# Gate, up and convolution matmuls as ordered 64-row pairs on TensorE, with norm statistics split between VectorE and GpSimd

## The chip, the cores and the metric

The kernel runs on one core of a Trainium2 chip. A core has TensorE (PE, matmuls; its weight loads are listed apart as PEld), VectorE (DVE), ScalarE (ACT), GpSimd (POOL), and SyncE (SP), from whose queue nearly all transfers are issued. The metric is the device time of one execution in microseconds (us), lower is better.

## The reference

For 2048 rows of 576 numbers in bfloat16, the reference computes an adaptive-norm block with a long convolution, and then a gated feed-forward part:

```python
mod = (silu(c) @ w_mod).reshape(1, 6, 1, -1)        # sa, ca, ga, sb, cb, gb
h = layernorm(q) * (1 + ca) + sa
kv = shift(k, shift_k) * v                          # four taps per channel
y = irfft(rfft(kv, 4096) * rfft(ssm_k, 4096))[:2048] + kv * ssm_D
x = q + ga * (h * y)
h = layernorm(x) * (1 + cb) + sb
x = x + gb * ((silu(h @ w1) * (h @ w3)) @ w2)       # w1, w3: 576 x 4608, w2: 4608 x 576
```

The Fourier transforms are the reference's way to a causal convolution over the 2048 positions, one filter per channel. The norms have no weights of their own, and divide by sqrt(variance + 1e-5).

## The kernel before

**Tiling.** The rows are cut into eight blocks of 256 for the convolution (`s` = 0 to 7) and four blocks of 512 for the feed-forward part (`r` = 0 to 3; block r holds convolution blocks 2r and 2r+1). The convolution is done by blocks: short Fourier transforms of each block of kv (`X`) and of the filter (`V`, from spectra `W`) as matmuls with a cosine and sine basis, products and sums of spectra on VectorE (`pair`, L403), and an inverse transform by matmuls (`inverse`, L533). Spectra that are needed again later are written to DRAM by `keep_x` and `keep_v` (L418, L422) and read back by `get` (L433); all of these are issued from SP.

**Feed-forward.** The 4608 hidden columns are 36 tiles of 128, taken in nine chunks of four (`fc`). The contraction over 576 channels is four tiles of 128 rows and one of 64 rows. An item is one hidden tile over 512 rows (or two hidden tiles over 256 rows): gate and up products go into the two banks of one PSUM tile, ScalarE takes silu of the first (L939) and copies the second (L941, tile `u`), and VectorE multiplies them into `h` (L942, all three in `hide`). The PSUM pool has four such tiles in rotation, and the convolution takes its own PSUM tiles from the same pool (`ps`, L70). The remaining 64 rows of w1 and w3 lie in one weight tile, w1's in partitions 0 to 63 and w3's in 64 to 127[...].

**`stream`** (L885) runs the gate and up products for r = 0, 1 and 2, in pairs of items: the 16 matmuls of 128 rows of the early item (`full`), its two 64-row matmuls (`rest`), the two 64-row matmuls of the late item, and the 16 of 128 rows of the late item. After each item `advance` (L874) lets the convolution of the next row block come in, piece by piece. It is a chain of generators, each piece yielding what it is supposed to cost; a budget grows with every item by a rate derived from `CONV_US` (72, 97 and 108 us for r = 0, 1, 2). A negative yield is a distance that other pieces are to fill (`mix`, L721). Before r = 0's stream stands the first block, written out in order (`first_block`, L632); then `stream` runs 24 hidden tiles on the first 256 rows with block 1's convolution beside it (`conv_second`, L781), then the rest of r = 0.

**`stream_halves`** (L975) runs r = 3, which has no convolution beside it. Every matmul has 64 rows. A pair is one matmul on rows 0 to 63 into one bank and one on rows 64 to 127 into the other; after five pairs the banks are swapped, and four pairs follow. Both halves of the rows thus accumulate in each bank, one after the other. The swapped part of an item runs after the first part of the next item, and its order behind the first part is kept by a memset on GpSimd that waits for the first part and is waited for by the second:

```python
nc.gpsimd.memset(self.tok[:], 0.0)          # L993
marks[f] = newest()
self.wait_for(marks[f], first)
```

**`down`** (L1014) multiplies h by w2 for each row block and adds into the output rows.

**Weights.** `load_w13` (L865) loads one chunk of w1 and w3: two transfers of 512 KB and two of 64 KB. Two buffers alternate, and a load waits until the chunk before last has been used.

**Norm statistics.** ScalarE makes the sums and the sums of squares (`ln_sums`, L441); `ln_scales` (L455) turns them into a scale and a shift for each row in five small operations, all on GpSimd. `gate_stats` (L488) does this for the first norm, `ln_stats` (L447) for the second. `normed_act` (L566) then writes the normed rows, `turn` (L573) transposes them on TensorE, and `turned` (L597) brings them to the feed-forward's input. `k_rows` (L359) transposes the filter rows in the same way.

**Order.** The instructions stand on each engine in the order in which the program issues them, except where `behind` (L483) or `issue_after` places one behind another. Waits between engines are by semaphore.

## Time and profile before

The three runs took 521.01, 521.48 and 522.43 us.

| | us |
|---|---|
| median of three runs | 521.48 |
| profiled execution, whole | 520.93 |
| profiled execution, span | 518.7 |
| TensorE busy | 498.0 |
| TensorE weight loads busy | 295.0 |
| VectorE busy | 339.7 |
| ScalarE busy | 294.1 |
| GpSimd busy | 72.0 |
| gate and up, 128-row matmuls (L920), 1056 | 200.7 |
| gate and up, 64-row matmuls beside them (L931), 264 | 33.1 |
| gate and up of r = 3, 64-row matmuls (L987), 648 | 70.3 |
| down matmuls (L1032), 1152 | 146.7 |

The granted TensorE clock was 0.996 on the mean. The span is from the first to the last recorded instruction; 2.2 us of the profiled execution lie around it. Busy times of matmuls are of overlapping instructions, so that the mean of one is longer than the distance from one to the next. In the lines of the timeline and of the chain, the columns are start in us, duration in us, engine, line and operation, the output tile and its inputs, and `x16` for a run of sixteen; `[1.03 <-ACT u L941]` says that the engine stood idle for 1.03 us before, until the instruction named.

### The profile page before, as it was taken

Reading aid. Unit: us, or ns where it says so; the run is one execution under the profiler, and the core shown is the slowest. Engines: PE = TensorE matmul, PEld = TensorE weight load, DVE = VectorE, ACT = ScalarE, POOL = GpSimd, SP = SyncE. Lnnn points to the kernel's source line nnn. Section 1 sums busy time; section 2 is a strip of 40 time slices with the busy share of each in tenths; the row PEclk is TensorE's granted clock in tenths of the full one; section 3 lists DMA queues with packets and bytes.
Section 4 is the critical chain, followed back from the end, with each engine's and each line's share of the span. In section 5 each row is a group of like instructions: output and inputs, shape, how many; then the busy total and the mean of one; then the engine's idle time right before and its main releaser. Section 6 shows DMA issues by size and latency. Waiting matters only on the chain.

```text
span 518.7 us, 9266 instructions
## 1 busy us (share of the span) xinstructions
PE 498.0 (96%) x3650; PEld 295.0 (57%) x3650; DVE 339.7 (65%) x515; ACT 294.1 (57%) x581; POOL 72.0 (14%) x131
## 2 busy tenths in 40 slices
PE   6998999988899999999999999999999999999996
PEld 3666875455587544444677643434578644444775
DVE  8897899997895445798999636999761222222012
ACT  5757789665652367858643465886725355555000
POOL 3304005107012001100102000530101000000000
PEclk9999999999899999999999999999999999999999
DMA  8947869678679966467997649855555545532462
GB/s 273 321 148 207 265 226 285 198 249 255 198 233 322 299 194 224 112 233 252 368 300 243 183 124 365 309 184 141 156 138 141 157 122 161 174 115 71 117 180 69
DMA packets 102206, 107.80 MB, mean 208 GB/s; under 512 B 5075, under 2 KB 94228, under 8 KB 102164
## 3 DMA queue, kind: packets, MB, share of 16 engines
q1 hardware_dynamic: 102142, 107.21, 66.3%
q8 instruction: 28, 0.46, 0.4%
q14 instruction: 14, 0.11, 0.1%
q10 hardware_dynamic: 22, 0.01, 0.0%
HBM read 96.00 MB, written 11.21 MB: 207 GB/s over the span
## 4 chain that ended last, share of the span: by engine, by line
PE 69%; DVE 17%; DMA 5%; ACT 4%; POOL 2%; issue 1%; SPq 0%; POOLq 0%; ACTq 0%
PE ps L1032 25%; PE ps L920 20%; PE ps L987 12%; DMA wst<-in_B_w_dram 4%; PE ps L931 3%; DVE p L413 2%; DVE z L415 2%; DVE h L942 2%; PE ps L302 2%; POOL l2v L460 2%; PE ps L543 2%; DVE kv L338 1%; PE ps L316 1%; ACT junk L445 1%; DVE kvt L337 1%
## 5 line engine op out<-in xcount | busy, mean ns | idle before, releaser
L920 PE MATMUL ps<-h2T,wst 128*128 128x512 bf16 (+1 forms) x1056 | 200.7, 341 | 1.0 <-ACT W L318 0.8
L1032 PE MATMUL ps<-wst,h 128*128 128x288 bf16 x1152 | 146.7, 288 | 2.4 <-ACT u L941 1.2
L920 PEld LDWEIGHTS <-wst 128*128 128x128 bf16 x1056 | 100.2, 98 | 85.8 <-issue 14.0
L1032 PEld LDWEIGHTS <-h 128*128 128x128 bf16 x1152 | 112.9, 98 | 33.0 <-issue 3.9
L939 ACT ACTIVATE h<-ps 128x512 bf16<-128x512 f32 x108 | 64.9, 601 | 69.1 <-PE ps L931 41.9
L942 DVE TENSOR_TENSOR h<-h,u 128x512 bf16<-128x512 bf16 x108 | 45.0, 421 | 42.2 <-ACT u L941 42.2
L987 PE MATMUL ps<-h2T,wst 64*128 64x512 bf16 x648 | 70.3, 376 | 0.2 <-DMA wst<-in_B_w_dram 0.2
L941 ACT CAST u<-ps 128x512 bf16<-128x512 f32 x108 | 63.4, 587 | 0.0
L413 DVE TENSOR_TENSOR p<-X,V 128x3456 bf16<-128x3456 bf16 x28 | 54.7, 1954 | 8.9 <-DMA X<-Xd 6.4
L415 DVE TENSOR_TENSOR z<-z,p 128x3456 bf16<-128x3456 bf16 x28 | 54.7, 1954 | 0.2
L987 PEld LDWEIGHTS <-wst 64*128 64x128 bf16 x648 | 31.4, 94 | 38.9 <-DMA wst<-in_B_w_dram 0.7
L1002 DVE TENSOR_TENSOR h<-h,u 128x512 bf16<-128x512 bf16 x36 | 15.3, 425 | 55.4 <-ACT u L1001 55.4
L1049 DVE TENSOR_TENSOR og<-ps,gbrow 128x288 bf16<-128x288 f32 x32 | 13.2, 450 | 48.8 <-PE ps L1032 48.8
L999 ACT ACTIVATE h<-ps 128x512 bf16<-128x512 f32 x36 | 21.5, 598 | 36.6 <-PE ps L987 36.6
L445 ACT ACTIVATE junk<-x 128x576 bf16<-128x576 bf16 x54 | 37.1, 688 | 0.5
L460 POOL TENSOR_TENSOR l2v<-l2s 128x2 f32<-128x2 f32 x6 | 14.7, 2456 | 156.4 <-ACT junk L445 156.4
L460 POOL TENSOR_TENSOR l1v<-l1s 128x2 f32<-128x2 f32 x7 | 17.8, 2544 | 127.3 <-ACT junk L445 127.3
L931 PE MATMUL ps<-h2T,wst 64*128 64x512 bf16 (+1 forms) x264 | 33.1, 342 | 0.0
L605 ACT ACTIVATE h2T<-ps,sbcol,cbcol 128x256 bf16<-128x256 bf16 x35 | 16.8, 570 | 23.4 <-PE ps L575 23.4
L570 ACT ACTIVATE h2row<-x,l2n,l2r 128x576 bf16<-128x576 bf16 (+1 forms) x24 | 13.8, 652 | 17.1 <-POOL l2n L464 17.1
L1001 ACT CAST u<-ps 128x512 bf16<-128x512 f32 x36 | 20.9, 580 | 0.0
L931 PEld LDWEIGHTS <-wst 64*128 64x128 bf16 x264 | 8.5, 94 | 21.2 <-issue 20.8
(142 smaller groups left out, 431.0 us busy)
## 6 DMA issues: line engine op xcount, KB each, us to landing
wst<-in_B_w_dram SPq DMA_DIRECT2D x80, 512.0 KB, 5.0
wst<-in_B_w_dram SPq DMA_DIRECT2D x72, 288.0 KB, 3.6
X<-Xd SPq DMA_DIRECT2D x8, 864.0 KB
Xd<-X SPq DMA_DIRECT2D x6, 864.0 KB, 6.1
wst<-in_B_w_dram SPq DMA_DIRECT2D x80, 64.0 KB, 3.0
kh<-in_A_k_dram SPq DMA_DIRECT2D x7, 720.0 KB, 7.2
Vd<-V SPq DMA_DIRECT2D x4, 864.0 KB
V<-Vd SPq DMA_DIRECT2D x4, 864.0 KB, 8.4
```

The lines of the kernel that those rows point to most:

```text
L413: nc.vector.tensor_mul(p[:], X[:], V[:])
L415: nc.vector.tensor_add(z[:], z[:], p[:])
L445: self.nc.scalar.activation(junk[:], src[:, i, :], func, scale=scale, accum_out=out[:, col:col + 1])
L460: e.tensor_mul(var[:], ssum[:], ssum[:])
L920: nc.tensor.matmul(gus[k][:, i, a * n:(a + 1) * n], w[:, 5 * i + ct, (fi + a) * P:(fi + a + 1) * P], hT[:, ct, t0:t1], start=(first and ct ...
L931: nc.tensor.matmul(gus[k][:, i, a * n:(a + 1) * n], w[rows, 4, (fi + a) * P:(fi + a + 1) * P], hT[rows, 4, t0:t1], start=(first and a == 0 ...
L939: nc.scalar.activation(h3, gus[k][:, 0, :].rearrange("p (a t) -> p a t", a=m), ACT.Silu)
L941: nc.scalar.copy(u[:], gus[k][:, 1, :])
L942: nc.vector.tensor_mul(h3, h3, u[:].rearrange("p (a t) -> p a t", a=m))
L987: nc.tensor.matmul(gus[f][:, i, :], w[rows, 5 * i + ct if ct < 4 else 4, cols], hT[rows, ct, :], start=swap == 0 and ct == 0, stop=swap == ...
L999: nc.scalar.activation(h3, gus[f][:, 0, :], ACT.Silu)
L1032: nc.tensor.matmul(acc[t], self.h3[:, f0 + f, t * P:(t + 1) * P], w[:, f, :], start=(f0 + f == 0), stop=(f0 + f == NF - 1))
```

## The change

Gate and up products of all four row blocks now run in `stream`, as pairs of 64-row matmuls; `stream_halves` and the GpSimd memset are gone. An item is a first part of five pairs and, with the banks swapped, a second part of four (`part`). The first two pairs (`AHEAD`) of the next item are issued between them. The second part waits for the last matmul of the first by TensorE's own semaphore: `after` puts a no-operation with that dependency on TensorE and places the following matmul behind it.

While a stream runs (`halves` is true) the convolution's matmuls run as such pairs too (`two_banks`): first all terms with rows 0 to 63 into one bank and rows 64 to 127 into the other, then the same swapped, behind a wait. In between, `pause` ends the present round of `advance`, so that part of an item comes in between. `advance` is called twice an item, with half the budget each. The transposes of filter rows and of normed rows become 64 by 64 transposes, two for each of 128 rows, into two banks, and the copies out of PSUM follow that layout; the filter rows need two copies instead of one. In the first block and beside the down products the former 128-row matmuls remain.

The norm's small operations are split. `ln_var` makes the variance with two VectorE operations and leaves the power to GpSimd; `ln_shift` makes the shift with one VectorE operation, and is called later. The new calls of `gate_var` stand after the filter or kv pieces.

Left out of the diff below: the removed bodies, which are shown above, constants that are not used any more, and calls whose arguments alone change.

```diff
+AHEAD = 2
...
+    def newest(self):
+        return self.nc.cur_bb.bb.instructions[-1]
+
+    def after(self, first):
+
+        with self.behind(self.nc.tensor):
+            nop = self.nc.tensor.nop().ins
+            self.tc.add_manual_dep(
+                nop, first.name,
+                mybir.DependencyInfo(mybir.DependencyClass.Sync, mybir.DependencyReason.DATA),
+                reason="both halves of the rows write this bank, one after the other")
+        return self.tc.issue_after(nop)
+
+    def two_banks(self, outs, terms):
+
+        mm = self.nc.tensor.matmul
+        if not self.halves:
+            for n, term in enumerate(terms):
+                for i in range(2):
+                    mm(outs[i], *term(i, slice(0, P)), start=(n == 0), stop=(n == len(terms) - 1))
+            return
+        for swap in range(2):
+            with self.after(mark) if swap else nullcontext():
+                for n, term in enumerate(terms):
+                    for rows, i in ((slice(0, 64), swap), (slice(64, P), 1 - swap)):
+                        mm(outs[i], *term(i, rows), start=(swap == 0 and n == 0),
+                           stop=(swap == 1 and n == len(terms) - 1))
+            if swap == 0:
+                mark = self.newest()
+                self.pause = True
+                yield 0.0
...
+                def term(cc):
+                    return lambda h, rows: (basis[rows, cc * (e + 1), cs], rhs[rows, cc, h * H:(h + 1) * H])
                 ps = self.ps()
-                for cc in range(2):
-                    for h in range(2):
-                        nc.tensor.matmul(ps[:, h, 0:H], basis[:, cc * (e + 1), cs],
-                                         rhs[:, cc, h * H:(h + 1) * H],
-                                         start=(cc == 0), stop=(cc == 1))
+                yield from self.two_banks([ps[:, h, 0:H] for h in range(2)], [term(cc) for cc in range(2)])
...
+        if self.halves:
+            for cc in range(2):
+                for ct in range(5):
+                    for half in range(2 if ct < 4 else 1):
+                        rows, at = slice(64 * half, 64 * half + 64), 320 * cc + 64 * ct
+                        nc.tensor.transpose(pt[:, half, at:at + 64], nat[rows, ct, cc:B:2],
+                                            self.ident[rows, rows])
+            for half, n in ((0, 5), (1, 4)):
+                nc.scalar.copy(_ap(kT, 64 * half, [[D, 2], [P, n], [1, 64]]),
+                               _ap(pt, 1024 * half, [[320, 2], [64, n], [1, 64]]))
+        else:
+            for cc in range(2):
+                for ct in range(5):
+                    nc.tensor.transpose(pt[:, cc, ct * P:(ct + 1) * P], nat[:, ct, cc:B:2],
+                                        self.ident[:])
+            nc.scalar.copy(kT[:], pt[:, :, 0:D])
...
-    def ln_stats(self, src, name):
-
-        ssum = self.small.tile([P, 2], F32, name=name + "s", tag="ssum")
-        ssq = self.small.tile([P, 2], F32, name=name + "q", tag="ssq")
-        for i in range(2):
-            self.ln_sums(src, i, ssum, ssq)
-        return self.ln_scales(ssum, ssq, name)
-
-    def ln_scales(self, ssum, ssq, name):
-        small = self.small
+    def ln_var(self, ssum, ssq, name):
         n = ssum.shape[-1]
-        var, rstd, nmr = [small.tile([P, n], F32, name=name + k, tag=f"ln{k}{n}") for k in "vrn"]
-        e = self.nc.gpsimd
+        var, rstd = [self.small.tile([P, n], F32, name=name + k, tag=f"ln{k}{n}") for k in "vr"]
+        e = self.nc.vector
         e.tensor_mul(var[:], ssum[:], ssum[:])
-        e.tensor_sub(var[:], ssq[:], var[:])
-        e.tensor_single_scalar(var[:], var[:], EPS, op=ALU.add)
-        e.tensor_tensor(rstd[:], var[:], self.neghalf[:, 0:n], op=ALU.pow)
-        e.tensor_mul(nmr[:], ssum[:], rstd[:])
+        e.scalar_tensor_tensor(var[:], ssq[:], EPS, var[:], op0=ALU.add, op1=ALU.subtract)
+        self.nc.gpsimd.tensor_tensor(rstd[:], var[:], self.neghalf[:, 0:n], op=ALU.pow)
+        return ssum, rstd, name
+
+    def ln_shift(self, ssum, rstd, name):
+        n = ssum.shape[-1]
+        nmr = self.small.tile([P, n], F32, name=name + "n", tag=f"lnn{n}")
+        self.nc.vector.tensor_mul(nmr[:], ssum[:], rstd[:])
         return rstd, nmr
...
+        self.l1[s] = ssum, ssq, "l1"
+
+    def gate_var(self, s):
+        self.l1[s] = self.ln_var(*self.l1[s])
 
     def gate_rows(self, s):
 
         x1 = self.xo[s]
-        r, b = self.l1.pop(s)
+        r, b = self.ln_shift(*self.l1.pop(s))
...
+            for half in range(2):
+                rows, at = slice(64 * half, 64 * half + 64), 320 * cc + 64 * ct
+                self.nc.tensor.transpose(pt[:, half, at:at + 64], self.h2row[rows, cc, cols],
+                                         self.ident[rows, rows])
...
-                    r, b = self.ln_stats(self.xo[s], "l2")
-                yield -waits[2]
+                    for i in range(2):
+                        self.ln_sums(self.xo[s], i, *sums)
+                yield -waits[2] / 2
+                stats = self.ln_var(*sums, "l2")
+                yield -waits[2] / 2
+                r, b = self.ln_shift(*stats)
...
         yield from self.v_block(1)
+        self.gate_var(1)
         yield from self.pair(self.X[0], self.V[1], 1)
...
             yield from self.kv_rows(s0)
+            self.gate_var(s0)
...
             yield from self.pair(X0, self.V[s1], s1)
+            self.gate_var(s1)
             self.gate_rows(s0)
...
+            if self.pause:
+                self.pause = False
+                break
...
+        def part(k, swap, some=slice(None)):
             (fc, t0, t1, _, _), fi, m = items[k]
             w, n = ws[fc, t0, t1], t1 - t0
+            terms = [(ct, a) for ct in ((0, 1, 2, 3) if swap else (4, 0, 1, 2, 3)) for a in range(m)]
+            for ct, a in terms[some]:
+                cols = slice((fi + a) * P, (fi + a + 1) * P)
+                for rows, i in ((slice(0, 64), swap), (slice(64, P), 1 - swap)):
                     nc.tensor.matmul(gus[k][:, i, a * n:(a + 1) * n],
-                                     w[rows, 4, (fi + a) * P:(fi + a + 1) * P], hT[rows, 4, t0:t1],
-                                     start=(first and a == 0), stop=(not first and a == m - 1))
+                                     w[rows, 5 * i + ct if ct < 4 else 4, cols], hT[rows, ct, t0:t1],
+                                     start=swap == 0 and (ct, a) == terms[0],
+                                     stop=swap == 1 and (ct, a) == terms[-1])
+            return self.newest()
...
+            if k == len(items):
+                return
             if items[k][1] == 0:
                 load(items[k][0])
             gus[k] = self.ps()
-        for k in range(0, len(items), size):
-            early, late = range(k, k + size // 2), range(k + size // 2, k + size)
-            for m in early:
-                begin(m)
-                full(m, True)
-            for m in early:
-                rest(m, False)
-            for m in late:
-                begin(m)
-                rest(m, True)
-            for m in early:
-                hide(m)
-            if finish and late.stop == len(items):
+            part(k, 0, slice(0, AHEAD * items[k][2]))
+        self.halves = True
+        begin(0)
+        for k in range(len(items)):
+            if finish and k + 1 == len(items):
                 self.end()
-            for m in late:
-                full(m, False)
-                hide(m)
-
-    def wait_for(self, later, first):
-
-        self.tc.add_manual_dep(
-            later, first.name,
-            mybir.DependencyInfo(mybir.DependencyClass.Sync, mybir.DependencyReason.DATA),
-            reason="both halves of the rows write this bank, one after the other")
-
-    def stream_halves(self, r):
-
-        nc = self.nc
-        hT = self.h2T[r % 2]
-        newest = lambda: nc.cur_bb.bb.instructions[-1]
-        gus, ws, marks = {}, {}, {}
-
-        def part(f, swap):
-            w = ws[f // FC]
-            cols = slice(f % FC * P, (f % FC + 1) * P)
-            for ct in range(4 if swap else 5):
-                for rows, i in ((slice(0, 64), swap), (slice(64, P), 1 - swap)):
-                    nc.tensor.matmul(gus[f][:, i, :], w[rows, 5 * i + ct if ct < 4 else 4, cols], hT[rows, ct, :],
-                                     start=swap == 0 and ct == 0, stop=swap == 1 and ct == 3)
-                    if swap == 1 and ct == 0 and i == 1:
-                        self.wait_for(newest(), marks.pop(f))
-            if swap == 0:
-                first = newest()
-                nc.gpsimd.memset(self.tok[:], 0.0)
-                marks[f] = newest()
-                self.wait_for(marks[f], first)
-
-        def hide(f):
-            h3 = self.h3[:, f, :]
-            nc.scalar.activation(h3, gus[f][:, 0, :], ACT.Silu)
-            u = self.hp.tile([P, RB], BF16, name="u", tag="u")
-            nc.scalar.copy(u[:], gus.pop(f)[:, 1, :])
-            nc.vector.tensor_mul(h3, h3, u[:])
-        for f in range(NF + 1):
-            if f < NF:
-                if f % FC == 0:
-                    self.load_w13(f // FC, (r + f // FC) % 2)
-                    ws[f // FC] = self.w13.pop(f // FC)
-                gus[f] = self.ps()
-                part(f, 0)
-            if f > 0:
-                part(f - 1, 1)
-                hide(f - 1)
+            mark = part(k, 0, slice(AHEAD * items[k][2], None))
+            self.advance(rate * 2.05 * 0.5)
+            begin(k + 1)
+            with self.after(mark):
+                part(k, 1)
+            hide(k)
+            self.advance(rate * 2.05 * 0.5)
+        self.halves = False
...
-            if r == NRB - 1:
-                self.stream_halves(r)
-            else:
-                self.stream(r, jobs, rate, 2)
+            self.stream(r, jobs, rate)
```

## The prediction

> **What bounds the kernel now.** I read the page's busy shares first, then the windows by stage, the chain of waits, and the timeline around the places that change. The page:

> ```profile
> span 518.7 us, 9266 instructions
> PE 498.0 (96%) x3650; PEld 295.0 (57%) x3650; DVE 339.7 (65%) x515; ACT 294.1 (57%) x581; POOL 72.0 (14%) x131
> ```

> TensorE is busy 96% of the span, but 96% is a mean. The windows by stage (columns: stretch, its length, then PE, PEld, DVE, ACT and POOL busy, granted clock, DMA share, GB/s), for most of the r=0 stream, then all of the r=1, r=2 and r=3 streams:

> ```profile
> 65.50:127.00 61.50, 57.86 (x436) 35.57 (x436) 61.11 (x83) 45.53 (x93) 18.59 (x12) 1.00 0.76 238
> 167.00:252.00 85.00, 84.16 (x451) 37.07 (x450) 59.05 (x84) 60.18 (x121) 6.35 (x15) 1.00 0.72 233
> 291.00:372.00 81.00, 80.20 (x417) 33.74 (x416) 59.97 (x84) 55.25 (x110) 11.97 (x11) 1.00 0.65 213
> 408.60:479.00 70.40, 70.16 (x650) 31.38 (x648) 16.15 (x41) 37.06 (x70) 3.17 (x36) 1.00 0.44 134
> ```

> In r=0 it is VectorE that is full (61.11 of 61.5); TensorE has 3.6 us to spare. In r=1 and r=2 TensorE is full and VectorE has over 20 us to spare. r=3 already runs as 64-row pairs.

> The chain of waits gives the price of an item in both forms:

> ```profile
> 215.60 3.56 PE ps L920 x16
> 219.70 3.56 PE ps L920 x16
> 223.79 3.56 PE ps L920 x16
> 431.61 47.66 PE ps L987 x440
> ```

> In r=1 two items take 223.79 - 219.70 = 4.09 us, 2.05 us each. In r=3, 220 pairs take 47.66 us, 216.6 ns a pair, so an item of nine pairs takes 1.95 us. The lines of the 128-row matmuls leave 4.09 - 3.56 = 0.53 us for two pairs (0.43 us) and 0.10 us over. The start-to-start times there show the 0.10: 96 ns at each change between 128-row and 64-row work, and little else.

> [...] a two-element multiply on POOL took 8.21 us while VectorE was full:

> ```profile
> 118.66 8.21 POOL L460 TENSOR_TENSOR l2v<-l2s 128x2 f32<-128x2 f32 x1 [25.81 <-ACT junk L445]
> 127.53 0.72 POOL L463 TENSOR_TENSOR l2r<-l2v,neghalf 128x2 f32<-128x2 f32 x1
> 128.56 2.29 ACT L570 ACTIVATE h2row<-x,l2n,l2r 128x576 bf16<-128x576 bf16 x4 [6.36 <-POOL l2n L464]
> 131.85 0.75 PE L367 MATMUL ps<-ident,knat 128*128 128x128 bf16 x10 [4.29 <-ACT u L941]
> ```

> **Part 1: mode changes go.** Between 33 and 372 us I count 56 changes into 64-row work at 96 ns (5.4 us) and as many back: 10.7 us, about 3.2 in r=0, 3.5 in r=1, 3.5 in r=2. In r=0 they lie under VectorE: worth 0 (3.2 if VectorE were not full). In r=1 and r=2 they lie on the path: -7.0.

> **Part 2: the wait of TensorE on itself.** A matmul's update comes 391 ns after its start (512 columns) and a waiting weight load goes 42 ns later: 0.43 us in all. In the new order two pairs of the next item (AHEAD = 2) and any piece of convolution stand between the mark and the waiting part, 0.55 to 0.77 us of work. So it costs 0; what queues behind it is all of TensorE. Were it late by 73 ns on each of some 144 items, it would eat all 10.7 us. For the first part of a convolution pair `yield 0.0` with `pause` puts half an item in between: 0 too.

> **Part 3: PSUM tiles come back later.** This is the charge that the change does not announce. The pool has four tiles in rotation. Before, an item's tile was asked for again with over 2 us of TensorE work in between. Now the lead pairs of item k+2 are issued right after the first part of k+1, and a convolution piece is let in at every half item; where item, convolution, item, convolution alternate, the tile for the lead of k+2 is that of item k. Between the last matmul of item k and that lead stand three pairs (0.65 us) and two half pieces of convolution (0.48 us at 120 ns a 288-column pair): 1.11 to 1.13 us. What has to happen meanwhile: matmul end 0.39, ScalarE's start 0.06, silu to cast 0.49 (below), cast 0.58, release 0.04, in all 1.55 us. The wait is 0.44 us.

> ```profile
> 300.50 0.60 ACT L939 ACTIVATE h<-ps 128x512 bf16<-128x512 f32 x1 [0.94 <-PE ps L920]
> 300.99 0.58 ACT L941 CAST u<-ps 128x512 bf16<-128x512 f32 x1
> ```

> Going through the new order tile by tile: six such places in r=1 and one of 0.19, 2.8 us; in r=2 two of 0.44 and four of 0.19 to 0.32, 1.7 us; in r=0 3.1 us, hidden by VectorE. Where ScalarE also runs a statistics pass (0.69 us) in front, more: up to 2 us. I take +4.5 (bounds 3 to 8).

> **Part 4: weights are wanted sooner.** The lead of the next chunk's first item needs w1 and w3 both, before the last part of the present chunk; before, w1 alone was needed first, and w3 some 0.9 us later. The window from release to need shrinks by 1.9 us. A chunk lands 5.9 us after its release, 7.7 with a spilled V before it on SP's queue, 9.2 with an X between. In r=1 one or two chunks fall short: +1 (0 to 2). In r=2 SP's queue now stands so:

> ```profile
> 307.83 1.11 SPq L872 DMA_DIRECT2D wst<-in_B_w_dram  x2
> 308.99 0.58 SPq L438 DMA_DIRECT2D X<-Xd  x1
> 309.67 0.93 SPq L871 DMA_DIRECT2D wst<-in_B_w_dram  x2
> 310.65 0.88 SPq L438 DMA_DIRECT2D V<-Vd  x1
> ```

> In the new order two chunks have an X and a V (864 KB each) ahead of them, where now one X lies between: 3.4 us later at these rates. The path allows for part of it; +3 (0 to 8). Against it, TensorE's 1.5 us of idle time at 370 to 372 us, behind ScalarE's statistics, may shrink: -0.5.

> **Part 5: r=0.** VectorE sets the pace. The four tiles of block 1's spectrum are now spread over item halves (2.1 us in one go before, about 5.9), which puts VectorE idle by some 4 us before the X sums. GpSimd's 8.21 us at 118.66 becomes three VectorE operations of 0.15 us and one power of 0.7: up to 4.3 us gained at 131.85, the wait shown above. But VectorE waits for the power, as the next tiny multiply stands right behind (0.8 us, some five times), and once its first multiply stands about 2.5 us ahead of ScalarE's sums. I take +0.8 for the stage (-2 to +7).

> **Part 6: small things.** Half transposes, 18 or 20 of 64x64 where 10 full ones took 0.56 us: -0.3 to +0.3 a set; kT copied by two ScalarE passes in place of one of 1.13 us: +0.3 in all. First block: ScalarE's wait for GpSimd's statistics (2.2 us) goes, but TensorE holds the path there: -0.3. r=3: the GpSimd memset that ordered the halves cost nothing (it waited with 1.8 us to spare); -0.2. The down stages are untouched.

> **The sum.** -7.0 + 4.5 + 1 + 3 - 0.5 + 0.8 + 0.3 - 0.3 - 0.2 = +1.6, and +0.5 as a share of the ScalarE collisions of part 3 that I could not place: +2.1. The profiled execution took 520.93 us, of which 518.7 is the span; it lies 0.55 under the median of 521.48. 521.48 + 2.1 = 523.6; I forecast 523.5 us.

> **The rivals.**
> (a) Faster. [...] PSUM waits at their low end (3), no DMA wait, -2 in r=0: -7.0 + 3 - 0.5 - 2 - 0.2 = -6.7, about 515. It decides once weights arrive in the shorter window (parts 4 under 1 us), and r=0 keeps its POOL gain. For it: the 96 ns are real, and DMA share is 0.65 to 0.72 in r=1 and r=2. Against: the rotation of four tiles is arithmetic.
> (b) No change. VectorE and ScalarE hold r=0 and the end of r=2 (the chain of waits runs over VectorE from 341 to 366 us), so that the gain lives in r=1 alone and the PSUM waits eat it: -3.5 + 2.8 + 0.5 = about 521.3.
> (c) Much slower. A late chunk in r=2 delays items, these delay u and h, VectorE's products start late, and the end of the stream moves with them; with +8 for DMA and +5 in r=0: about 531. For it: at 332.98 the chain already holds 2.02 us of waiting for weights.
> [...]

> **How the numbers follow.** Chances: my forecast with its neighbourhood (+0.3% to +1%, 523 to 527) 0.35, (a) 0.27, (b) 0.20, (c) 0.18. About 0.3% (1.6 us) is what a measurement of this kernel can tell from no change. Slower: 0.35 + 0.18 = 0.53; same 0.20; faster 0.27. The likeliest case's own range is 522 to 527; the range over all cases is 515.5 to 530: it leaves out about one in ten below, where (a) comes with all its gains, and one in ten above.

> **What would show it.** Right: items in r=1 without a convolution beside them at 1.95 us; the 96 ns steps gone; some ten TensorE waits of 0.2 to 0.5 us released by the cast of u in r=1 and r=2; a TensorE wait on weights in r=2 near 315 to 335 us; no POOL operation of several us in the statistics. Wrong: TensorE waits in r=1 and r=2 under 2 us in all (then a), or waits of the second parts on TensorE itself, which I put at 0, or VectorE in r=0 idle by more than 5 us (then c).

## The result, and the profile after

The changed kernel takes 572.12 us (569.82 to 574.86 over four runs) where the kernel before takes 521.25 us in the same comparison: 1.098 times as long (95% interval 1.092 to 1.103). The forecast was 523.5 us in a range from 515.5 to 530; its direction was right, its size was not.

One sentence of the description above has to be corrected. On the engines the instructions do not simply stand in the order in which the program issues them: outside the first block a scheduler of the framework sorts them by its own reckoning of when each can start, and only what `behind`, `issue_after` or a data dependency ties down stays. That matters below.

The page of the changed kernel:

```profile
span 570.0 us, 11683 instructions
PE 506.5 (89%) x4891; PEld 323.4 (57%) x4892; DVE 347.7 (61%) x557; ACT 297.6 (52%) x586; POOL 21.6 (4%) x39
```

TensorE's share falls from 96% to 89%, while its matmuls at full clock take the same time (table below). GpSimd's busy time falls from 72.0 to 21.6 us, as meant. The windows of the four streams, with the columns of the table of before:

```profile
65.50:155.00 89.50, 69.43 (x932) 49.78 (x926) 72.62 (x112) 56.77 (x114) 4.65 (x5) 0.92 0.60 189
196.00:284.00 88.00, 78.51 (x733) 40.60 (x731) 56.68 (x90) 59.47 (x118) 2.06 (x3) 0.98 0.61 197
331.00:423.00 92.00, 80.83 (x733) 41.05 (x730) 62.63 (x93) 57.93 (x115) 2.06 (x3) 0.94 0.55 181
460.60:530.00 69.40, 69.40 (x644) 31.10 (x645) 15.96 (x40) 37.32 (x70) 0.00 (x0) 1.00 0.45 136
```

In r=0 VectorE is no longer full (72.6 of 89.5), in r=1 and r=2 TensorE has 9 to 11 us of gaps, and its granted clock is 0.92 to 0.98 in all three. Only r=3 is as good as before. TensorE's waits by line and releaser (us in all, times, longest), the five largest that concern the streams and the down stages:

```profile
PE ps L983 <- ACT u L995: 16.5, 16, 3.6
PE ps L983 <- DMA wst<-in_B_w_dram: 11.8, 9, 1.8
PE ps L618 <- DVE h2row L518: 6.7, 3, 5.2
PE ps L1038 <- DMA wst<-in_B_w_dram: 5.5, 3, 4.8
PE ps L97 <- ACT u L995: 4.3, 4, 1.7
```

Before, no wait of TensorE in r=1 and r=2 came to 1 us.

From the start of each matmul (a pair counted as one) to the start of the next, less the matmul's own time (the median at full clock from one such matmul to the next in these two traces: 216 ns for 512 columns, whether one 128-row matmul or a pair of 64 rows, and 122 in the one and 123 in the other for 288), the span divides as follows, to about 1 us. "Half clock" is time lost where a matmul takes twice its time (427 ns for a pair of 512 columns, 240 for 288 columns), in the stretches where the trace shows a granted clock of one half and at the very start; "waits" are gaps over 0.15 us; a change of mode is one between 128-row and 64-row matmuls.

| us | before | after | difference |
|---|---|---|---|
| matmuls at full clock, and other short gaps | 475.2 | 473.5 | -1.7 |
| waits | 17.2 | 67.6 | +50.4 |
| half clock | 4.7 | 17.9 | +13.2 |
| changes of mode (150 before, 50 after) | 14.3 | 4.6 | -9.7 |
| ahead of the first and after the last matmul | 7.3 | 6.4 | -0.9 |
| span | 518.7 | 570.0 | +51.3 |

So the change does what it says: 100 of 150 changes of mode are gone. It pays for that with 64 us of waits and half clock. By stage, each bounded by the first or last w2 matmul (r=0's stream from 33 us on), in us:

| | r=0 stream | down | r=1 stream | down | r=2 stream | down, r=3 and its down |
|---|---|---|---|---|---|---|
| before | 99.8 | 41.0 | 78.2 | 39.5 | 78.5 | 144.4 |
| after | 122.0 | 41.0 | 86.8 | 47.8 | 90.2 | 145.4 |

How a wait in r=1 comes about, on TensorE and on ScalarE of the changed kernel (timeline):

```profile
229.89 0.30 PE L97 MATMUL ps<-kv,Fb 64*128 64x288 bf16 x2
230.47 1.47 PE L983 MATMUL ps<-h2T,wst 64*128 64x512 bf16 x12 [0.27 <-ACT u L995]
232.53 0.30 PE L97 MATMUL ps<-kv,Fb 64*128 64x288 bf16 x2
235.06 2.74 PE L983 MATMUL ps<-h2T,wst 64*128 64x512 bf16 x12 [2.23 <-ACT u L995]
```

```profile
230.83 0.71 ACT L487 ACTIVATE junk<-x 128x576 bf16<-128x576 bf16 x1
...
233.27 0.68 ACT L487 ACTIVATE junk<-x 128x576 bf16<-128x576 bf16 x1
...
233.96 0.58 ACT L993 ACTIVATE h<-ps 128x512 bf16<-128x512 f32 x1
234.43 0.57 ACT L995 CAST u<-ps 128x512 bf16<-128x512 f32 x1
```

At 230.47 the lead of an item waits for the PSUM tile of the item before last; from the start of the matmul ahead (229.89) it is 0.58 us, 0.45 more than that matmul takes. At 235.06 four passes of norm statistics stood on ScalarE ahead of silu and cast, and the same wait is 2.4 us. Then the twelve matmuls take 2.74 us in place of 1.47: the granted clock is 0.50 from 234.91 to 238.32 us.

In this trace the clock is 1.00 or 0.50 wherever it is recorded, from 9.6 us on. Up to the last matmul there are ten stretches at 0.50, eight of 3.41 us and two of 6.83 us, and their starts lie whole multiples of 3.41 us apart. Cut into steps of 3.41 us from one of these starts, the two traces have 297 whole steps at full clock, the kernel before from 12.9 us on and the changed one from 9.6 us. In 11 of them, one before and ten after, TensorE was idle (no matmul in the profile) for 1.92 us or more, and each was followed by a step at half clock; in the other 286 it was idle for 1.78 us or less, and none was. The length of a single wait did not tell. A wait of 2.02 us in the kernel before, 1.17 and 0.85 us of it in two steps, was not followed by half clock (first line); one of 1.68 us in the changed kernel, in a step with 1.92 us of idle time in all, was (second line, then the windows of that step and the next):

```profile
44.51 0.77 PE L302 MATMUL ps<-kv,Fb 128*128 128x288 bf16 x5 [2.02 <-DVE kv L340]
```

```profile
130.84 0.30 PE L97 MATMUL ps<-kv,Fb 64*128 64x288 bf16 x2 [1.68 <-ACT u L995]
```

```profile
129.10:132.51 3.41, 1.49 (x22) 1.02 (x21) 3.41 (x5) 1.67 (x3) 0.00 (x0) 1.00 1.08 350
132.51:135.92 3.41, 3.41 (x24) 1.71 (x20) 3.41 (x4) 1.62 (x3) 0.00 (x0) 0.50 0.65 193
```

### The profile page after: what moved, and what is told of

Same layout as the page of the kernel before. It is cut to its first block, busy times and chain, and to the rows that moved or that the text cites. A ratio compares the mean times of both kernels' runs of the same rounds, so it can differ in the third digit from the quotient of the medians.

```text
span 570.0 us, 11683 instructions
## 1 busy us (share of the span) xinstructions
PE 506.5 (89%) x4891; PEld 323.4 (57%) x4892; DVE 347.7 (61%) x557; ACT 297.6 (52%) x586; POOL 21.6 (4%) x39
## 4 chain that ended last, share of the span: by engine, by line
PE 53%; DVE 19%; DMA 14%; ACT 10%; issue 2%; SPq 1%; POOL 0%; DVEq 0%; ACTq 0%; POOLq 0%
PE ps L983 29%; PE ps L1038 19%; DMA wst<-in_B_w_dram 9%; ACT junk L487 4%; DVE p L455 4%; DVE z L457 3%; DMA h<-in_w_mod_dram 2%; ACT u L995 2%; DVE h L996 2%; DVE kvt L368 2%; ACT h L993 2%; PE ps L91 2%; DVE kv L369 1%; DMA kh<-in_A_k_dram 1%; PE ps L284 1%
## 5 line engine op out<-in xcount | busy, mean ns | idle before, releaser
L983 PE MATMUL ps<-h2T,wst 64*128 64x512 bf16 (+1 forms) x3024 | 311.0, 357 | 32.1 <-ACT u L995 16.5
L983 PEld LDWEIGHTS <-wst 64*128 64x128 bf16 x3024 | 166.1, 97 | 158.1 <-issue 33.2
L1055 DVE TENSOR_TENSOR og<-ps,gbrow 128x288 bf16<-128x288 f32 x32 | 13.2, 451 | 44.9 <-PE ps L1038 44.9
L97 PE MATMUL ps<-kv,Fb 64*128 64x288 bf16 x128 | 18.0, 302 | 4.8 <-DVE l1v L494 3.1
L368 DVE TENSOR_TENSOR kvt<-kh,shk 128x1152 bf16<-128x1152 bf16 x24 | 18.1, 753 | 6.4 <-DMA kh<-in_A_k_dram 6.3
L97 PEld LDWEIGHTS <-Fb 64*128 64x128 bf16 x208 | 12.6, 99 | 13.9 <-issue 8.2
L800 ACT CAST y<-ps 128x576 bf16<-128x576 f32 x14 | 8.8, 645 | 20.9 <-PE ps L91 20.7
L369 DVE TENSOR_TENSOR kv<-kv,kvt 128x1152 bf16<-128x1152 bf16 x24 | 18.1, 753 | 0.3
L349 ACT CAST X<-ps 128x576 bf16<-128x576 f32 x24 | 15.7, 653 | 0.4 <-PE ps L97 0.4
L450 DVE TENSOR_TENSOR z<-X,V 128x3456 bf16<-128x3456 bf16 x7 | 13.7, 1954 | 3.2 <-DMA X<-Xd 3.1
L495 POOL TENSOR_TENSOR l2r<-l2v,neghalf 128x2 f32<-128x2 f32 x6 | 6.2, 1035 | 218.3 <-DVE l2v L494 218.3
L365 DVE TENSOR_TENSOR kv<-kh,shk 128x1152 bf16<-128x1152 bf16 x8 | 6.0, 755 | 11.8 <-DMA kh<-in_A_k_dram 8.1
```

Source lines behind the costliest of these rows:

```text
L97: mm(outs[i], *term(i, rows), start=(swap == 0 and n == 0), stop=(swap == 1 and n == len(terms) - 1))
L368: nc.vector.tensor_mul(tmp[:], kh[:, 3 - j:5 - j, :], tap(j))
L369: nc.vector.tensor_add(kv[:], kv[:], tmp[:])
L983: nc.tensor.matmul(gus[k][:, i, a * n:(a + 1) * n], w[rows, 5 * i + ct if ct < 4 else 4, cols], hT[rows, ct, t0:t1], start=swap == 0 and ( ...
```

## The experiments

The stage lengths of the runs that are compared below, in us; waits and half clock are sums over the run as in the first table (left out for two runs whose traces lack some matmuls). Two measures of noise: the medians of the kernel before, taken beside each of these runs, lie between 520.0 and 521.7 us; and a_self, which is the changed kernel up to r=3, has 123.0, 85.4 and 89.1 us in the three streams where the changed kernel has 122.0, 86.8 and 90.2. A stage that differs by 1.5 us or less says nothing.

| run | median | r=0 stream | r=1 stream | down r=1 | r=2 stream | waits | half clock |
|---|---|---|---|---|---|---|---|
| before | 521 | 99.8 | 78.2 | 39.5 | 78.5 | 17.2 | 4.7 |
| after | 572.1 | 122.0 | 86.8 | 47.8 | 90.2 | 67.6 | 17.9 |
| b_ln | 519.0 | 95.7 | 78.2 | 43.6 | 79.0 | 14.7 | 6.0 |
| a_kv2 | 564.8 | 115.1 | 86.7 | 47.3 | 91.6 | 63.4 | 16.0 |
| a_late | 561.9 | 116.3 | 85.7 | 44.8 | 91.2 | 57.5 | 18.3 |
| a_full | 559.5 | 114.4 | 85.4 | 47.6 | 88.2 | 48.4 | 14.9 |
| a_nolead | 565.3 | 115.1 | 83.0 | 47.7 | 89.6 | 58.6 | 16.8 |
| a_all | 556.0 | 112.4 | 83.5 | 48.8 | 87.4 | 54.6 | 13.3 |
| a_all_full | 550.2 | 104.1 | 85.3 | 45.7 | 87.0 | 40.5 | 7.5 |
| a_order | 548.2 | 100.3 | 89.1 | 43.8 | 93.2 | 38.9 | 11.6 |
| b_psum3 | 527.5 | 99.7 | 81.0 | 39.3 | 82.7 | | |
| b_pause | 540.3 | 110.8 | 78.2 | 49.3 | 78.2 | | |
| b_best | 516.5 | 95.5 | 78.4 | 39.1 | 79.1 | 15.3 | 3.5 |

### The split of the norm statistics

The edit puts `ln_var`, `ln_shift` and the calls of `gate_var` of the change into the kernel before, and nothing else.

```diff
-        self.l1[s] = self.ln_scales(ssum, ssq, "l1")
+        self.l1[s] = ssum, ssq, "l1"
+
+    def gate_var(self, s):
+        self.l1[s] = self.ln_var(*self.l1[s])
```

> The kernel before with the split of the norm statistics alone (two VectorE operations, the power on GpSimd, one VectorE operation later, at the same places as in the changed kernel). Theory 'the split is small': VectorE waits 0.8 us for the power at some five to ten places, GpSimd's 8 us operation goes: 517 to 524 us. Theory 'the split is a main cause, since TensorE waits behind it': 530 us or more.

518.98 us, ratio 0.9973 (0.9956 to 0.9991): the split is a small gain. r=0's stream is 4.1 us shorter, the stage where GpSimd's 8.21 us operation stood, and the down stage of r=1 is 4.1 us longer. The reverse, the changed kernel with the statistics on GpSimd:

```diff
-        e = self.nc.vector
+        e = self.nc.gpsimd
...
-        self.nc.vector.tensor_mul(nmr[:], ssum[:], rstd[:])
+        self.nc.gpsimd.tensor_mul(nmr[:], ssum[:], rstd[:])
```

> The changed kernel with the norm statistics all on GpSimd as before, the undo of the second part of the change alone. Theory 'the split costs where buffers are short': 558 to 568 us. Theory 'the split is a gain here as in the kernel before (0.3%)': 572 to 577 us.

573.1 us against 572.1: no difference. The split is not the cause.

### One order on VectorE

The orders of VectorE's instructions in the two programs, around block 1's residual (number, line, operation). First the kernel before, then the changed one:

```
82 L942 TensorTensor h_102<-h_102,u 128x2x256 x2
83 L557 TensorTensor hg<-hg,y 128x1152
84 L558 TensorTensor x_314<-x_314,hg 128x1152

85 L996 TensorTensor h_101<-h_101,u 128x2x256 x2
86 L365 TensorTensor kv<-kh,shk 128x1152
87 L368 TensorTensor kvt<-kh,shk 128x1152
88 L996 TensorTensor h_101<-h_101,u 128x2x256
89 L594 TensorTensor hg<-hg,y 128x1152
```

Nothing in the diff asks for it, but the scheduler has put block 2's taps (L365) ahead of block 1's residual (L594). On the chip the keys `kh` were late, since their load stands behind weight chunks that were late themselves. VectorE of the changed kernel (timeline):

```profile
65.49 0.43 DVE L996 TENSOR_TENSOR h<-h,u 128x512 bf16<-128x512 bf16 x1 [3.06 <-ACT u L995]
74.04 0.76 DVE L365 TENSOR_TENSOR kv<-kh,shk 128x1152 bf16<-128x1152 bf16 x1 [8.13 <-DMA kh<-in_A_k_dram]
...
75.72 0.75 DVE L594 TENSOR_TENSOR hg<-hg,y 128x1152 bf16<-128x1152 bf16 x1
```

Eight us of the engine that sets the pace of r=0. The edit ties the taps of block 2 (`row1` is the last instruction that writes block 1's normed rows), in both tap products:

```diff
-        nc.vector.tensor_mul(kv[:], kh[:, 3:5, :], tap(0))
+        with self.tc.issue_after(self.row1) if s == 2 else nullcontext():
+            nc.vector.tensor_mul(kv[:], kh[:, 3:5, :], tap(0))
```

> The changed kernel with one order restored: VectorE's tap products of block 2 stand behind the normed rows of block 1, as in the kernel before. Theory 'order on VectorE': the changed kernel's VectorE stood 8.1 us on the keys' transfer with block 1's residual queued behind it, and TensorE stood 5.4 + 1.5 us for the normed rows; both go, some 8 us less and part of the half-clock stretch after it: about 562 us. Theory 'PSUM and weights': this is only one of many waits, the streams stay as late, 570 to 572 us.

564.83 us: 7.3 us less, all of it in r=0's stream (122.0 to 115.1), as expected of the first theory.

### Weights at the start of a chunk

```diff
-            part(k, 0, slice(0, AHEAD * items[k][2]))
+            if items[k][1] > 0:
+                part(k, 0, slice(0, AHEAD * items[k][2]))
```

> The changed kernel, but the first item of each weight chunk has no lead pairs: it starts after the second part of the item before, so that the chunk is wanted about 1.9 us later. Theory 'weights are wanted too soon': the 11.8 us of TensorE waits on weights in the streams and the half-clock stretches behind them go, 558 to 564 us. Theory 'PSUM tiles and the convolution': the weights were late because TensorE itself was late, so little changes, and the second part now waits 0.2 to 0.4 us for the first at some 40 chunks: 568 to 582 us.

561.85 us: 10.3 us less, as the first theory has it. The waits on weights in r=0's first stream, 6.2 us, are gone, and the stage is 5.7 us shorter. TensorE now stands there 2.7 us for the input of block 1's inverse, which it did not before.

### The convolution in one go

```diff
-        self.halves = True
         begin(0)
```

> The changed kernel with gate and up as 64-row pairs, but the convolution's matmuls and transposes beside them in 128 rows, each tile at one go, as before. About 90 convolution tiles bring two changes of mode each at 96 ns: 17 us if nothing hides them, about 5 in each of r=1 and r=2. Theory 'the convolution cut in halves is what costs' (its tiles take PSUM buffers for longer and come later to VectorE): 545 to 555 us in spite of the mode changes. Theory 'gate and up with their lead cost by themselves': 575 to 585 us.

559.49 us: 12.6 us less, but not the 17 to 27 that the first theory asked for. Most of it is r=0's (7.6 us). In r=1 and r=2 it is 1.4 and 2.0 us shorter, hardly more than the noise, with nearly as many mode changes as before the change (146 in the run). In r=0 the lateness of weights and of kv is still there.

### PSUM tiles and statistics passes

The next kernel drops the lead pairs wherever a convolution piece has just been issued, so that a PSUM tile is asked for about 1 us later:

```diff
-            begin(k + 1)
+            begin(k + 1, AHEAD if self.newest_on(nc.tensor) is mark else 0)
```

> The changed kernel, but the next item gets lead pairs only where no convolution piece has just been issued; elsewhere its tile is asked for after the second part of the item before, so that 9 pairs and two half pieces (2.2 us) lie between an item's end and the next use of its PSUM tile in place of 1.1 us. The second part then waits for the first over a convolution half alone, 0.43 - 0.22 - 0.12 = 0.1 us a time. Theory 'PSUM tiles come back too late': the 0.45 us waits and the waits of 2 us behind a statistics pass in r=1 and r=2 go, with the half-clock stretches: r=1 from 86.8 to about 81, r=2 from 90 to about 83, in all 550 to 558 us. Theory 'ScalarE and VectorE are late by themselves': TensorE waits for them at the second part or at the next tile just as long, 568 to 574 us.

565.33 us. In r=1, where the prediction had put six waits of 0.44 us, the stream falls from 86.8 to 83.0; in r=2 only from 90.2 to 89.6. The sum lies between the two theories: the first one is right for a part of r=1 (3.8 us of some 6), and r=2's gain is within the noise. The statistics passes one by one, with a `pause` after each of the four:

```diff
+                with self.behind(self.nc.scalar):
+                    self.ln_sums(self.xo[s], i, ssum, ssq, only=one)
+                self.pause = self.halves
+                yield 0.4
```

> The changed kernel with the four ScalarE passes of each block's norm statistics let in one per half item, where now two or four stand in a row. Theory 'a run of statistics passes on ScalarE meets the short PSUM slack': the 2 us waits become 0.5 us ones[...]: 560 to 566 us. Theory 'the statistics only mark where VectorE and ScalarE were late anyway': 570 us and over, as the norm ends later.

567.30 us: r=2 gains (90.2 to 84.8), r=0 loses (125.3), r=1 is unchanged within the noise (88.0). The two theories are not told apart by the sum; the lesson is only that moving these passes moves the wait.

A control in the kernel before takes one of its four PSUM tiles away during r=1 and r=2, with nothing else of the change in it:

```diff
+                hold = self.ps() if r else None
...
                 self.stream(r, jobs, rate, 2)
...
+                        self.nc.scalar.copy(self.held[:], hold[:, 0, 0:1])
```

> The kernel before with one of the four PSUM tiles withheld during the streams of r=1 and r=2 (a column is written into it ahead of the stream and read after it). Nothing else is changed: 128-row matmuls, no lead, no halves. Theory 'the loss in r=1 and r=2 is PSUM slack': TensorE waits on ScalarE appear in both streams, 8 to 12 us each with half-clock stretches after the longer ones: 535 to 545 us. Theory 'the loss comes from the halves and the lead': three tiles do for this order, 520 to 526 us.

527.52 us, ratio 1.012 (1.008 to 1.016); r=1 +2.8, r=2 +4.2 us, and TensorE waits of up to 1.2 us for ScalarE's cast that were not there before. So one tile less costs the old order some 7 us in these two streams, less than half of what was expected, and of the 20 us that they lost by the change. The result lies between the ranges of the two theories. It is a stand-in: the change has four tiles and asks for them sooner.

### TensorE waiting on itself

```diff
-            part(k, 0, slice(0, AHEAD * items[k][2]))
+            part(k, 0, slice(0, lead * items[k][2]))
+        lead = 0 if r == NRB - 1 else AHEAD
```

> The changed kernel with no lead pairs in r=3 alone, where nothing else runs on TensorE: the second part of each of 36 items waits for the first with nothing in between. If a wait of TensorE on itself costs 391 + 42 ns less the 216 ns that a pair takes anyway, 36 x 0.22 = 7.8 us; if it costs the whole 0.43, 15.6 us; r=3 then takes 77 or 85 us in place of 69.3. A rival that says that the wait is free without a lead: 69 us.

r=3's stream takes 77.5 us in place of 69.3: 8.2 us, 0.23 for each of 36 items, the smaller of the two figures. With the lead, r=3 shows no such wait (the window above: TensorE busy 69.40 of 69.40).

### The chain of the convolution, drawn out

The change lets a convolution tile in by halves, with half an item in between. Block 1's inverse transform on TensorE, before:

```profile
56.98 2.15 PE L543 MATMUL ps<-z,Fb 128*128 128x288 bf16 x16
```

and in the kernel a_all (below), whose other losses in this stage are smaller, with what it means for VectorE:

```profile
60.63 1.45 PE L100 MATMUL ps<-z,Fb 64*128 64x288 bf16 x8 [2.58 <-DVE z L568]
63.99 2.15 PE L100 MATMUL ps<-z,Fb 64*128 64x288 bf16 x16
67.25 0.67 PE L100 MATMUL ps<-z,Fb 64*128 64x288 bf16 x8
```

```profile
68.56 0.42 DVE L1002 TENSOR_TENSOR h<-h,u 128x512 bf16<-128x512 bf16 x1 [6.53 <-ACT u L1001]
69.11 0.76 DVE L599 TENSOR_TENSOR hg<-hg,y 128x1152 bf16<-128x1152 bf16 x1
```

What took TensorE 2.2 us before now takes from 60.63 to 67.92, in part at half clock: the granted clock is 0.83 on the mean from 55 to 75 us (in the changed kernel itself it takes 4.2 us, from 64.17 to 68.41), and VectorE, with the product and then the residual next in its queue, stands idle for 6.5 us. A control in the kernel before keeps its 128-row matmuls and whole tiles, and only lets its convolution tiles in one per item (a break after each tile of a spectrum and of an inverse):

```diff
+                self.pause = self.instream
+                yield 0.0
...
+            if self.pause:
+                self.pause = False
+                break
```

> The kernel before with its convolution tiles let in one per item at most (a break after every tile of a spectrum and of an inverse transform), matmuls and everything else as they are. The spectrum of block 1 and the inverse of every block, in one go before, are then spread over items of 2 us. Theory 'drawn-out chains make VectorE wait': r=0's stream, where VectorE is full, grows from 99.8 to 105 to 110 us, r=1 and r=2 stay within 1 us: 525 to 531 us. Theory 'VectorE has other work to do meanwhile': 520 to 523 us.

540.31 us, ratio 1.037 (1.034 to 1.041), more than the first theory gave. Block 1's inverse takes 4.2 us from its first matmul to its last, as in the changed kernel. r=0's stream grows by 11.0 us. VectorE's waits there (the kernel before, then b_pause, from 33 us to the stream's end):

```profile
DVE h L942 <- ACT u L941: 5.3, 2, 5.0
```

```profile
DVE h L951 <- ACT u L950: 16.9, 6, 5.3
```

r=1 and r=2 do not change, but the convolution is not done at the end of r=1, and the down stage after it has to wait, +9.8 us; in this kernel ScalarE is held there for 14.66 us by GpSimd's statistics:

```profile
302.26 2.29 ACT L574 ACTIVATE h2row<-x,l2n,l2r 128x576 bf16<-128x576 bf16 x4 [14.66 <-POOL l2n L468]
```

### The down stage of r=1

In the changed kernel it takes 8.3 us longer, 4.8 of them a wait for w2, whose transfers stood on SP's queue behind those for r=2. The edit turns that round:

```diff
-                    self.load_w13(fc, buf)
+                    with self.tc.issue_after(self.w2at[r - 1]) if fc < 2 else nullcontext():
+                        self.load_w13(fc, buf)
```

> The changed kernel with one order on SP's queue restored: the first two weight chunks of a later row block stand behind the sixth w2 transfer of the down stage before it. In the changed kernel they stood ahead, and the down stage of r=1 took 47.8 us in place of 39.5, with 4.8 us of TensorE waiting for w2 and a half-clock stretch. Theory 'the queue's order': that stage falls back to about 40 us, in all 563 to 566 us. Theory 'the transfers are too many, whatever the order': the wait moves to the first chunks of r=2, 569 to 573 us.

571.65 us: no gain. TensorE's waits from 280 to 330 us in this run:

```profile
PE ps L1042 <- DVE og L1059: 3.9, 1, 3.9
PE ps L1042 <- DMA wst<-in_B_w_dram: 0.4, 1, 0.4
```

The transfers were on time and TensorE then waited for VectorE, which still had the convolution before it. The order of the queue had only been the last of two. The time is in the second theory's range, but its reason is not what the trace shows. By this trace the stage is late because the convolution is; no run tests that alone.

### The edits together

The kernel a_all has the edits of a_kv2, a_late and a_nolead in one; the leads are then

```diff
+            led[k] = lead * items[k][2] if items[k][1] > 0 else 0
+            if led[k]:
+                part(k, 0, slice(0, led[k]))
```

> The changed kernel with three edits together: lead pairs only where no convolution piece was just issued, none for the first item of a weight chunk, and block 2's tap products behind the normed rows of block 1 on VectorE. If the three losses are separate, their gains add up: 572 - 7 (order) - 10 (weights) - 15 to -20 (PSUM): 535 to 541 us. If they are one loss seen at three places (each only moves the wait to the next thing that is late), 550 us or more.

Alone they gained 7.3, 10.3 and 6.8 us, together 16.1 (556.00 us) and not 24.4: the losses are in part one loss at several places. With the convolution whole besides, by the edit of a_full:

> The kernel with the three edits (lead only where no convolution piece was issued, none at a chunk's first item, block 2's taps behind block 1's rows) and, besides, the convolution in 128-row matmuls, each tile at one go. Theory 'cutting the convolution's tiles draws out its chains': block 1's inverse, 8.4 us from first matmul to second copy where it was 2.7, and the spectra come back in one go, VectorE's idle time in r=0 falls, r=0's stream from 112 to 103 to 106 us; the mode changes cost some 3 us in each of r=1 and r=2: 545 to 553 us. Theory 'r=0 is late for weights and statistics': 555 to 562 us.

550.20 us; r=0's stream falls from 112.4 to 104.1 as the first theory said, r=1 and r=2 do not gain (83.5 to 85.3, 87.4 to 87.0). Then the statistics back on GpSimd, by the edit of a_pool:

> Gate and up pairs alone: the kernel with the three edits and the convolution in 128-row matmuls (550 us), and besides the norm statistics all on GpSimd as before. In that kernel ScalarE waited 9.1 us in r=1 and 9.5 us in r=2 for VectorE to free a tile u, while VectorE stood in line for the statistics (2.4 + 1.7 + 1.7 us in r=1). Theory 'the split makes VectorE wait, and the short buffers pass it on to TensorE': r=1 from 85 to about 81, r=2 from 87 to about 82: 538 to 544 us. Theory 'the pairs and their mode changes beside 128-row tiles are what is left': 548 to 554 us.

561.61 us, 11.4 us more, which neither theory gave: r=1 and r=2 are unchanged (85.0 and 87.0), so the split is not what is left there; what comes back is a wait of TensorE of 11.2 us at the end of r=0, with ScalarE standing 12.9 us for GpSimd's statistics. Last, the place of the products h on VectorE:

```diff
-            self.advance(rate * 2.05 * 0.5)
+            with self.tc.issue_after(hs[-2]) if len(hs) > 1 else nullcontext():
+                self.advance(rate * 2.05 * 0.5)
```

> The same placing of the products, in the kernel with the three edits and the convolution whole in 128 rows (550 us), where ScalarE waited 9.1 us in r=1 and 9.5 us in r=2 for a tile u. Theory 'the order on VectorE is what is left in r=1 and r=2': 85 and 87 us go to about 80 (78.2 and 78.5 in the kernel before, and some 1.5 us more of mode changes): 535 to 541 us. Theory 'the pairs themselves': 548 to 553 us.

548.17 us, within 2 us of a_all_full: in the second theory's range, though not for its reason. r=0's stream is 100.3 us, as before the change (99.8). But r=1 and r=2 grow to 89.1 and 93.2. ScalarE of a_all_full waited there for a tile u (first line, from 309 to 400 us); in a_order that wait is gone, and TensorE waits for the convolution's input instead (second):

```profile
ACT u L1001 <- DVE h L1002: 9.5, 6, 3.6
```

```profile
PE ps L94 <- DVE kv L376: 7.2, 2, 3.8
```

The same edit in a_all and in the changed kernel itself:

> The same placing of the products, in the kernel with the three edits and the convolution in halves (556 us): the changed kernel with every loss mended that was found, but for the drawn-out chains of the convolution. Theory 'order on VectorE': 83.5 and 87.4 us in r=1 and r=2 go to about 79, 545 to 549 us in all; what is left over 521 us is then r=0 (112 against 99.8) and the end of the convolution in the down stage of r=1. Theory 'the halves themselves': 553 to 558 us.

> The changed kernel, with the convolution's VectorE operations of each half item placed behind the product h of the item before last, so that a product never stands behind more than some two items' worth of convolution. In the changed kernel the scheduler puts up to eight convolution operations ahead of a row of products, ScalarE then finds no free tile u (4.4 us in r=1, 4.4 in r=2) and does not release PSUM. Theory 'the order on VectorE holds up ScalarE': r=1 and r=2 lose 3 to 5 us each: 558 to 566 us. Theory 'it only shows that VectorE is late': 570 us and over, with the convolution later still.

561.55 and 577.66 us, 5.6 us more in each case. a_all_order misses both theories; a_hs is what its second theory said. By the traces, with products first the convolution is later, and TensorE, whose convolution matmuls have fixed places, waits for it.

### A version that beats both

The kernel before with the split, and with the convolution's VectorE operations beside r=1 and r=2 behind the products of the down stage before, for which TensorE had waited 2.6 us in b_ln:

```diff
-            self.advance(rate * 2.05)
+            with self.tc.issue_after(self.og0) if r in (1, 2) else nullcontext():
+                self.advance(rate * 2.05)
```

> The kernel before with the split of the norm statistics, and with the next convolution's VectorE operations that are let in beside r=1 and r=2 placed behind the first half's products of the down stage before. The split alone gained 4 us in r=0's stream and gave 4 back in the down stage of r=1, where TensorE waited 2.6 us for those products behind eight convolution operations on VectorE, with a half-clock stretch after it. Theory 'only that order gave it back': 514 to 516.5 us. Theory 'the gain in r=0 is lost again wherever the convolution ends': 518 to 520 us.

516.49 us, ratio 0.9924 (0.9899 to 0.9948). The down stage of r=1 is back at 39.1 us and r=0 keeps its gain.

## Why the prediction was wrong, step by step

**Part 1, mode changes: right.** In r=1 and r=2 they took 6.8 us before and 0.2 us after, where -7.0 was forecast; without its waits and half clock r=1's stream would take 86.8 - 11.8 - 1.5 = 73.5 us, 4.7 less than before. (An item over 512 rows had eight matmuls of 128 rows, not the 16 of the description; the `x16` lines run over two items, and the price of 2.05 us is right.)

**Part 2, TensorE's wait on itself: right.** 0 with the lead, 0.23 us an item without it.

**Part 3, PSUM: the mechanism right, a term mis-sized.** Six waits of 0.42 to 0.52 us stand in r=1, where six of 0.44 were forecast. The term "up to 2 us" for ScalarE's collisions is what failed: in r=1 and r=2 TensorE waits 14.7 us for the cast of u, and the six small ones are under 3 of them. Three waits behind four statistics passes each came to 8.8 us (2.4, 2.6 and 3.8). A second cause was not in the prediction at all: ScalarE itself waits 4.4 us around each of the two streams for a free tile u, because VectorE's products are late, and TensorE's two waits of 2.0 us for the cast stand there.

**Part 4, weights: right for r=1 and r=2** (1.5 and 2.3 us of waits, forecast 1 and 3), but r=0 was left out, where TensorE waited 8.0 us for them.

**Part 5, r=0: the step that failed most**, +0.8 forecast, with +7 as its upper end, and +22.2 measured. It charged 4 us of drawn-out chain to one spectrum and let it be made up for by GpSimd's 4.3. It did not follow the chain through the inverse transform and the later blocks (b_pause: +11.0 from such breaks), nor did it ask what stands next on VectorE when weights, and keys behind them, are late (a_kv2: 6.9). GpSimd's gain was real (b_ln: 4.1). Its own sign of being wrong came true: VectorE, which was to be idle by no more than 5 us, is idle for 16.9 of the 89.5 us of the window above. This step is the one that the runs settle best: with the three edits and the convolution whole r=0's stream takes 104.1 us, with the products placed first 100.3, against 122.0 and, before the change, 99.8 (95.7 with the split alone).

**What no part held: the half clock.** +13.2 us. Every wait was charged at its own length, though the trace of before has a stretch of 3.4 us at half clock after its 4.46 us wait.

**Part 6: "the down stages are untouched" was wrong.** That of r=1 grew by 8.3 us. r=3 with its down stage did not change (105.8 and 105.7 us).

Of the rivals, (c) had the sign and the mechanism, a delay that moves on from engine to engine, but added it up to 10 us. (a) and (b) are out.

What stays open is more than half of the loss. The edits together win back 22 to 24 of 51 us (550.20 and 548.17 us); of the 28 us that the trace of a_all_full still is longer than that of the kernel before, 4.3 stand in r=0, 7.1 in r=1, 6.2 in the down stage of r=1 and 8.5 in r=2. In r=1 and r=2 it is waits and half clock (8.1 and 9.6 us) and not the pairs' own matmuls, and it is not the split. With either order on VectorE one of its neighbours waits. More tiles u would tell more; this was not tried. Each edit also makes the scheduler sort anew (a_self alone kept its order), so that hardly any two of these kernels differ by their edit alone.

## What to carry to other kernels

Ask of a reordering first what slack it takes away and who lives on it: here TensorE was full in two of the streams, and PSUM tiles, weights and the convolution's chain all lived on slack that the new order uses up. Be wary of cutting a matmul that lies in another engine's serial chain into pieces that are spread over other work, above all where that other engine is the bound. Price a wait of TensorE of some 2 us or more with the half clock that may follow it, by an estimate from this case's matmul times (below) up to 1.7 us for each 3.41 us at half clock. And in a program whose order a scheduler fixes, compare the two orders on every engine and ask for each instruction that moved ahead what it waits for.

## What the runs showed of the hardware that was not expected

Thirteen GpSimd operations of one kind (L460, on two numbers a partition) took between 0.19 and 8.58 us in the kernel before. While the one of 8.21 us ran, VectorE was busy for 8.16 us:

```profile
118.66:126.87 8.21, 8.21 (x79) 6.45 (x78) 8.16 (x12) 3.55 (x8) 8.21 (x1) 1.00 0.92 291
```

One GpSimd operation on two numbers a partition took 14.71 us in a_pairs, with the next taking 0.20 us, and one took 12.68 us in b_pause:

```profile
125.56 14.71 POOL L498 TENSOR_TENSOR l2v<-l2s 128x2 f32<-128x2 f32 x1 [32.19 <-ACT junk L492]
140.35 0.20 POOL L499 TENSOR_TENSOR l2v<-l2q,l2v 128x2 f32<-128x2 f32 x1
```

```profile
289.55 12.68 POOL L468 TENSOR_TENSOR l2n<-l2s,l2r 128x2 f32<-128x2 f32 x1
```

ScalarE waited 12.9 us in a_pairs and 14.66 us in b_pause for the last of the statistics.
